# Running sums kept in PSUM between chunks by ScalarE copies, in place of VectorE adds in SBUF

## The chip, the cores and the metric

The kernel runs on one core of a Trainium2 chip, alone. The metric is device time in microseconds (us), the median of several executions; lower is better. The names of the engines in the profile are PE (TensorE, the matrix unit), DVE (VectorE), ACT (ScalarE), POOL (GpSimd) and SP (SyncE, which only issues transfers). A "q" behind a name (ACTq) is that engine's own instruction queue, which issues transfers and semaphore instructions.

## The reference

One layer of a network on x of 2048 rows and 576 columns. The rows are normalized, and two branches are added to x: a sliding, dilated attention and a two-layer MLP.

```python
xn = layernorm(x)
qkv = xn @ wqkv                      # 576 x 1728, 32 heads of 18
a = local_attention(qkv, window=8, dilation=2) @ wo
h = maximum(xn @ w1, 0)              # 576 x 4608
return x + a + h @ w2                # 4608 x 576
```

All of it is fp32. The kernel splits each operand into a high part and a rest (tiles hi and lo), both in a rounded fp32 form that the matrix unit takes at full rate, and multiplies three of the four pairs of parts.

## The kernel before, in words

The 2048 rows are taken in two phases of 1024. In a phase the rows lie in 8 tiles of 128 (index i), and two tiles make one of 4 row blocks (index tb). The 4608 hidden columns lie in 36 blocks of 128, and 3 blocks (index f) make one of 12 chunks (index c). A **slot** n is one (phase, c, tb, f), in this order from the outside in, so there are 288 slots, 144 in a phase, and f = n mod 3.

The tile X[phase, i] starts as x and collects every branch: it is the running sum, in SBUF. In slot n the main loop (lines 771 to 786) issues, in this order:

- run_splits(n): a part of a weight that has landed in SBUF is split by an ACT copy (hi) and a DVE subtraction (lo), lines 148 and 152;
- h_mm(n+2): the 14 matmuls of the first product two slots ahead, into a PSUM tile `ph`, and behind them h_out: an ACT relu into hhi (line 563) and a DVE operation that makes hlo (line 566);
- what the dictionary todo holds for slot n: tiles of the query, key and value product (qkv_tile), transposes of the next phase's x, the output projection of the attention (wo_b). The qkv_tile copies k, v and q out of PSUM on ACT (lines 397 to 399). The last of a unit's eight tiles also issues four transfers from ACT's queue (line 403), which copy the halo rows of k and v between partitions;
- o_mm(n): the 12 matmuls of the second product, 6 into PO[0] and then 6 into PO[1], one PSUM tile for each row tile of the block. Both tiles come from the pool ps_o, which has two buffers of two banks, so the next group's PO[0] lies where this group's lay;
- o_out(n), when f is 2: the three blocks of the chunk are summed in PO[0] and PO[1], and DVE adds each to its running sum (line 620);
- what todo_late holds, and run_bg: attention operations on DVE from a queue, as many as a count of planned DVE time (`t["dve"]`) against planned PE time (`t["pe"]`) admits. One of them is an exponential on ACT (line 444).

Each engine takes its instructions in the order in which the program issues them. Line 113 is the helper that issues every matmul, so the profile's rows of matmuls are told apart by their tiles: `ph` is the first product, `po` the second, `pm` the rest. A unit u of the attention has its eight qkv_tiles in slots 7+26u to 14+26u of each phase (u from 0 to 3). The attention's output projection lies in slots 127 to 137 of a phase; slots 139 to 143 of the first phase hold copies and subtractions (xt_s, lines 369 to 373) that split the next phase's x, which came back from memory transposed.

The last three slots write PO into other buffers and are finished in halves (lines 590 to 594 and 625 to 630).

Of the kernel before, what the change touches and what calls it, by code (L numbers as in the profile page):

```python
# [10 lines left out]
F32 = mybir.dt.float32  # L11
F32R = mybir.dt.float32r
AF = mybir.ActivationFunctionType
ALU = mybir.AluOpType
# [3 lines left out]
P = 128  # L18
# [7 lines left out]
C = 3  # L26
# [29 lines left out]
def tile_body(ctx: ExitStack, tc: tile.TileContext, x, wqkv, wo, w1, w2, out):  # L56
    nc = tc.nc
    S, D = x.shape
# [7 lines left out]
    D2 = D // 2  # L66
    CUT = (slice(0, 256), slice(256, D))
    scale = Dh ** -0.5
    SPC = NTB * C
# [20 lines left out]
    ps_o = pool("ps_o", 2, space=PSUM)  # L90
# [19 lines left out]
    t = {"pe": 0.0, "dve": 0.0}  # L110

    def mm(o, l, r, start, stop, n):
        nc.tensor.matmul(o, l, r, start=start, stop=stop)  # L113
        t["pe"] += n / 2400.0 + 0.002

    def dve(n):
        t["dve"] += (n + 130) / 960.0
# [119 lines left out]
    X, XT, XN, MR = {}, {}, {}, {}  # L237
# [144 lines left out]
    def qkv_tile(ph, u, i):  # L382
        if u == 0 and i == 0:
            QO[ph] = qop.tile([P, NI, D], F32, name="qo")
        if i == 0:
            assert len(bg) < 38, len(bg)
            KK[ph, u] = kp.tile([P, W - 1 + NI, UD], F32, name="k")
            VV[ph, u] = vp.tile([P, W - 1 + NI, UD], F32, name="v")
            nc.gpsimd.memset(KK[ph, u][0:1, 0 : W - 1, :], 0.0)
            nc.gpsimd.memset(VV[ph, u][0:1, 0 : W - 1, :], 0.0)  # L390
        k, v, wq = KK[ph, u], VV[ph, u], WQ[ph, u]
        tb, h = divmod(i, 2)
        xt = XT[ph, tb]
        pq = ps_m.tile([P, 3, UD], F32, name="pm")
        for j, (a, b) in enumerate(TERMS):
            mm(pq, xt[:, a, h * P : (h + 1) * P], wq[:, b, :], j == 0, j == len(TERMS) - 1, 3 * UD)
        nc.scalar.activation(k[:, W - 1 + i, :], pq[:, 1, :], AF.Copy)  # L397
        nc.scalar.activation(v[:, W - 1 + i, :], pq[:, 2, :], AF.Copy)
        nc.scalar.activation(QO[ph][:, i, u * UD : (u + 1) * UD], pq[:, 0, :], AF.Copy)
        if i == NI - 1:  # L400
            for z in (k, v):
                for a, b in HALO:
                    nc.scalar.dma_start(z[a + 1 : b + 1, 0 : W - 1, :], z[a:b, NI : NI + W - 1, :])
# [117 lines left out]
    def wo_b(ph, i):  # L521
        d, w = OT.pop((ph, i)), WO[ph]
        po = [ps_m.tile([P, c.stop - c.start], F32, name="pm") for c in CUT]
        for j, (a, b) in enumerate(TERMS):
            for h, c in enumerate(CUT):
                mm(po[h], d[a], w[b][:, c], j == 0, j == len(TERMS) - 1, D2)
        for h, c in enumerate(CUT):
            acc = X[ph, i][:, c]
            nc.vector.tensor_tensor(acc, po[h], acc, op=ALU.add)  # L529
            dve(D2)  # L530
# [3 lines left out]
    def done(ph, i):  # L534
        left[ph, i] -= 1
        if left[ph, i] == 0:
            nc.sync.dma_start(o_v[ph, i], X[ph, i])


    slots = [(ph, c, tb, f) for ph in range(NPH) for c in range(NCH) for tb in range(NTB) for f in range(C)]  # L540
    H, PO = {}, {}
# [3 lines left out]
    def h_terms(n, terms, other=False):  # L545
        ph, c, tb, f = slots[n]
        w, xt = W1[ph, c, f], XT[ph, tb]
        if n not in HP:
            HP[n] = ps_m.tile([P, TBN], F32, name="pm") if other else ps_h.tile([P, TBN], F32, name="ph")
            HN[n] = 0  # L550
        for a, b in terms:
            wb = w[:, b // 5, (b % 5) * P : (b % 5 + 1) * P]
            HN[n] += 1
            mm(HP[n], wb, xt[:, a, :], HN[n] == 1, HN[n] == len(TERMS), TBN)
# [24 lines left out]
    def half(po, h):  # L579
        if isinstance(po, list):  # L580
            return po[h]
        return po[:, 1, 0 : D - 256] if h else po[:, 0, 256:512]

    def o_mm(n, out=True, which=range(2)):
        ph, c, tb, f = slots[n]
        hi, lo = H[n]
        w = W2[ph, c, f]
        end = n == len(slots) - 1
        for k in which:
            if f == 0 and n == len(slots) - C:  # L590
                if k:
                    PO[k] = [ps_m.tile([P, c.stop - c.start], F32, name="pm") for c in CUT]
                else:
                    PO[k] = [ps_o.tile([P, 2, 512], F32, name="po")[:, 0, 0 : c.stop - c.start] for c in CUT]
            elif f == 0:
                PO[k] = ps_o.tile([P, 2, 512], F32, name="po")
            cs = slice(k * P, (k + 1) * P)
            terms = [(j, l, b, h) for j, (l, b) in enumerate(((hi, 0), (hi, 1), (lo, 0))) for h in range(2)]
            if end:
                terms.sort(key=lambda z: -z[3])  # L600
            for j, l, b, h in terms:
                mm(
                    half(PO[k], h), l[:, cs], w[:, b, CUT[h]],
                    f == 0 and j == 0, f == C - 1 and j == 2, D2,
                )
        if 1 in which:
            H.pop(n)
        if out:
            o_out(n, which)

    def o_out(n, which=range(2)):
        ph, c, tb, f = slots[n]
        if f < C - 1:
            return
        for k in which:
            i = 2 * tb + k
            acc = X[ph, i]
            if n < len(slots) - 1:
                whole = PO[k].rearrange("p b c -> p (b c)")[:, 256 : 256 + D]
                nc.vector.tensor_tensor(acc, whole, acc, op=ALU.add)  # L620
                dve(D)
                if c == NCH - 1:
                    done(ph, i)
                continue
            for h, c in reversed(list(enumerate(CUT))):
                nc.vector.tensor_tensor(acc[:, c], half(PO[k], h), acc[:, c], op=ALU.add)  # L626
                if k:
                    (nc.scalar if h else nc.sync).dma_start(o_v[ph, i][:, c], acc[:, c])
            if k == 0:
                done(ph, i)  # L630
# [13 lines left out]
    for ph in range(NPH):  # L644
        b = ph * SPP
# [93 lines left out]
    x2[1]()  # L739
    x2[3]()  # L740
    o_mm(0)
    o_mm(1)
    make_xt(0, 3, bank=ps_h)
    o_mm(2, out=False)
    stats(0, 4)
    s5 = stats(0, 5, parts=True)
# [6 lines left out]
    h4[0]()  # L753
    h4[1]()
    o_out(2, (0,))
    x4 = make_xt(0, 4, parts=True)
    for f in x4[:3]:
        f()
    norm(0, 5)
    o_out(2, (1,))  # L760
    x4[3]()
    h_terms(5, TERMS)
# [51 lines left out]
```

## Time and profile before

| | |
|---|---|
| time of the kernel, median of 3 runs (lowest, highest) | 1166.1 us (1165.38, 1167.42) |
| profiled execution, from its first to its last instruction | 1163.8 us |
| granted TensorE clock, mean | 0.999 |
| ACT copies and relus of 128x256 or more, from PSUM | 384 ns (256), 599 ns (512) |
| DVE add of a finished tile (line 620) | 190 of them, 757 ns each |

The profiled execution is one run with the hardware profiler on. Its page gives the span alone, 1163.8 us, so the median of the runs shown stands 2.3 us above it; what lies around the first and last instruction is in no row. A row of the timeline reads: start in us from the span's start, duration in us, engine, line, operation, written tile <- read tiles, shapes, count, and in brackets the idle time of the engine just before and what ended it. Where a row stands for several instructions, its duration runs from the first's start to the last's end. Matmuls overlap: the next starts before the last has ended, so the step from one group's start to the next is the time that counts. A row of a table of groups ends with: busy us, mean ns of one, idle us before them, and what ended that idle time.

### The profile page before, as it was taken

To read this page: it belongs to the slowest core of one execution; us is meant where nothing else is said; L and a number is where in the kernel's file an instruction comes from. 1 tells how busy PE (TensorE), PEld (TensorE's weight loads), DVE (VectorE), ACT (ScalarE), POOL (GpSimd) and SP (SyncE) were. 2 spreads that over 40 slices of the span, in tenths; PEclk is the share of its full clock that TensorE was granted. 3 is DMA by queue.
4 is the path that set the end of the run, shared out by engine and by line. 5 is a ranking of instruction groups with operands and counts; after the bars stand their busy time and mean duration, and the time that the engine had idled before them with its cause. 6 is when DMAs were issued, how large, how long until landed. Compare 5 with 4: busy or idle time off the path is not lost.

```text
span 1163.8 us, 21695 instructions
## 1 busy us (share of the span) xinstructions
PE 1155.9 (99%) x8916; PEld 1147.9 (99%) x8916; DVE 822.9 (71%) x1300; ACT 308.1 (26%) x747; POOL 44.9 (4%) x60
## 2 busy tenths in 40 slices
PE   8999999999999999999999999999999999999998
PEld 8999999999999999999999999999999999999998
DVE  7427885887687688876683288768858877887843
ACT  4422222131231212322433123222222312222210
POOL 2200100010000000000010001000100000000000
PEclk9999999999999999999999999999999999999999
DMA  6303221140321211365752113021312303113541
GB/s 184 98 23 85 65 55 53 40 112 1 94 76 34 82 32 52 96 151 116 175 170 66 46 53 94 22 77 36 92 34 62 110 1 101 44 32 97 123 100 63
DMA packets 149732, 88.66 MB, mean 76 GB/s; under 512 B 58512, under 2 KB 133264, under 8 KB 149632
## 3 DMA queue, kind: packets, MB, share of 16 engines
q1 hardware_dynamic: 146656, 78.54, 25.1%
q10 hardware_dynamic: 2976, 8.72, 2.6%
q8 instruction: 70, 1.15, 0.4%
q14 instruction: 30, 0.25, 0.1%
HBM read 67.90 MB, written 11.14 MB: 68 GB/s over the span
## 4 chain that ended last, share of the span: by engine, by line
PE 99%; issue 0%; DVE 0%; DMA 0%; POOL 0%; ACT 0%; SPq 0%; DVEq 0%; POOLq 0%
PE ph L113 39%; PE po L113 38%; PE pm L113 20%; PE pm L293 0%; DMA x<-in_x 0%; DVE x L626 0%; POOL rstd L264 0%; PE pm L294 0%; PE po L293 0%; ACT xT L298 0%; DVE xn L279 0%; DVE bst L257 0%; SPq L243 0%; DVEq L810 0%; PE ph L294 0%
## 5 line engine op out<-in xcount | busy, mean ns | idle before, releaser
L113 PE MATMUL ph<-xT,w1t 128*128 128x256 f32 x4018 | 505.0, 277 | 0.7 <-ACT xT L298 0.7
L113 PEld LDWEIGHTS ph<-xT,w1t 128*128 128x128 f32 x4018 | 486.8, 188 | 1.3 <-ACT xT L298 1.0
L113 PE MATMUL po<-w2t,hhi 128*128 128x256 f32 x2292 | 393.0, 293 | 0.0
L113 PEld LDWEIGHTS po<-w2t,hhi 128*128 128x128 f32 x2292 | 335.4, 188 | 1.1
L563 ACT ACTIVATE hhi<-ph 128x256 fp32r<-128x256 f32 x287 | 110.0, 384 | 582.2 <-PE ph L113 568.9
L113 PE MATMUL po<-w2t,hlo 128*128 128x256 f32 x1146 | 242.4, 292 | 0.0
L566 DVE SCALAR_TENSOR_TENSOR hlo<-ph,hhi 128x256 fp32r<-128x256 f32 x287 | 121.0, 422 | 164.5 <-ACT hhi L563 164.0
L113 PEld LDWEIGHTS po<-w2t,hlo 128*128 128x128 f32 x1146 | 188.9, 187 | 0.0
L620 DVE TENSOR_TENSOR x<-po,x 128x576 f32<-128x576 f32 x190 | 143.1, 757 | 60.1 <-PE po L113 57.2
L113 PE MATMUL pm<-wq,xT 128*128 128x432 f32 x896 | 185.5, 358 | 0.0
L113 PEld LDWEIGHTS pm<-wq,xT 128*128 128x128 f32 x896 | 163.8, 188 | 5.6
L428 DVE TENSOR_TENSOR pr<-qo,k 128x1152 f32<-128x1152 f32 x64 | 86.1, 1349 | 0.0
L431 DVE TENSOR_REDUCE lg<-pr 128x64 f32<-128x1152 f32 x64 | 85.1, 1343 | 0.0
L458 DVE TENSOR_TENSOR pr<-lg,v 128x1152 f32<-128x1152 f32 x64 | 84.7, 1350 | 0.0
L152 DVE TENSOR_TENSOR w2t<-st,w2t 128x576 fp32r<-128x576 f32 x72 | 55.8, 775 | 32.4 <-ACT w2t L148 32.3
L152 DVE TENSOR_TENSOR w1t<-st,w1t 128x640 fp32r<-128x640 f32 x70 | 58.9, 841 | 20.6 <-ACT w1t L148 20.5
L465 DVE TENSOR_TENSOR pr<-pr 128x288 f32<-128x288 f32 (+1 forms) x128 | 70.6, 601 | 0.0
L148 ACT ACTIVATE w2t<-st 128x576 fp32r<-128x576 f32 x72 | 49.3, 684 | 44.9 <-PE po L113 32.5
L397 ACT ACTIVATE k<-pm 128x144 f32<-128x144 f32 x64 | 18.7, 292 | 146.3 <-PE pm L113 146.3
L148 ACT ACTIVATE w1t<-st 128x640 fp32r<-128x640 f32 x71 | 52.1, 734 | 11.7 <-DMA k<-k 6.0
L434 POOL TENSOR_SCALAR_AFFINE_SELECT lg<-lg 1x512 f32<-1x512 f32 x8 | 9.9, 1234 | 809.6 <-DVE lg L431 809.6
L529 DVE TENSOR_TENSOR x<-pm,x 128x256 f32<-128x256 f32 (+1 forms) x32 | 13.1, 453 | 30.2 <-PE pm L113 30.2
(85 smaller groups left out, 470.0 us busy)
## 6 DMA issues: line engine op xcount, KB each, us to landing
st<-in_w SPq DMA_DIRECT2D x72, 288.0 KB, 3.1
st<-in_w SPq DMA_DIRECT2D x72, 256.0 KB, 3.2
st<-in_wqkv SPq DMA_DIRECT2D x32, 216.0 KB, 3.0
turned<-tr SPq DMA_DIRECT2D x64, 80.0 KB, 3.0
xn<-turned SPq DMA_DIRECT2D x16, 320.0 KB, 3.2
st<-in_w SPq DMA_DIRECT2D x142, 32.0 KB, 2.9
out<-x SPq DMA_DIRECT2D x15, 288.0 KB, 2.1
x<-in_x SPq DMA_DIRECT2D x14, 288.0 KB, 4.3
```

What stands on the lines that cost most here:

```text
L113: nc.tensor.matmul(o, l, r, start=start, stop=stop)
L148: nc.scalar.activation(hi, src, AF.Copy)
L152: nc.vector.tensor_tensor(lo, src, f32(hi), op=ALU.subtract)
L397: nc.scalar.activation(k[:, W - 1 + i, :], pq[:, 1, :], AF.Copy)
L428: nc.vector.tensor_tensor(pr[i], q, window(k, i), op=ALU.mult)
L431: nc.vector.tensor_reduce(lg[:, i], pr.pop(i).rearrange(heads, d=Dh), axis=AX.X, op=ALU.add)
L458: nc.vector.tensor_tensor(pr[i].rearrange(heads, d=Dh), e, window(v, i).rearrange(heads, d=Dh), op=ALU.mult)
L465: nc.vector.tensor_tensor(o, z[:, 0:n], z[:, n : 2 * n], op=ALU.add)
L529: nc.vector.tensor_tensor(acc, po[h], acc, op=ALU.add)
L563: nc.scalar.activation(hi, pt, AF.Relu)
L566: nc.vector.scalar_tensor_tensor(lo, pt, 0.0, f32(hi), op0=ALU.max, op1=ALU.subtract)
L620: nc.vector.tensor_tensor(acc, whole, acc, op=ALU.add)
```

## The change

Three things change. In the groups of slots from 12 to 284 the first matmul into PO no longer starts a new accumulation. The PSUM tile is written ahead by ACT: as soon as a group is finished, o_out takes the next group's PO[k] and copies the running sum of that group's row tile into it (the seed). And when a group is finished, ACT copies PO[k] back to the running sum (the copy back), where DVE added before. The order on ACT at a group's end is: copy back of k = 0, seed of k = 0, copy back of k = 1, seed of k = 1. The first chunk of the first phase and the last group keep their DVE adds: 182 of the 190 adds of line 620 go, and 182 copies back and 182 seeds come, at 91 ends of groups (slots 14 to 284 for the copies, 11 to 281 for the seeds). The planned DVE time of these adds leaves the count that run_bg uses.

```diff
-        nc.tensor.matmul(o, l, r, start=start, stop=stop)
+        nc.tensor.matmul(o, l, r, start=start, stop=stop, skip_group_check=True)
...
+    def seeded(n):
+        return SPC <= n < len(slots) - C
+
...
-            elif f == 0:
+            elif f == 0 and not seeded(n):
                 PO[k] = ps_o.tile([P, 2, 512], F32, name="po")
...
-                    f == 0 and j == 0, f == C - 1 and j == 2, D2,
+                    f == 0 and j == 0 and not seeded(n), f == C - 1 and j == 2, D2,
...
                 whole = PO[k].rearrange("p b c -> p (b c)")[:, 256 : 256 + D]
-                nc.vector.tensor_tensor(acc, whole, acc, op=ALU.add)
-                dve(D)
+                if seeded(n):
+                    nc.scalar.activation(acc, whole, AF.Copy)
+                else:
+                    nc.vector.tensor_tensor(acc, whole, acc, op=ALU.add)
+                    dve(D)
+                if seeded(n + 1):
+                    after = slots[n + 1]
+                    PO[k] = ps_o.tile([P, 2, 512], F32, name="po")
+                    whole = PO[k].rearrange("p b c -> p (b c)")[:, 256 : 256 + D]
+                    nc.scalar.activation(whole, X[after[0], 2 * after[2] + k], AF.Copy)
                 if c == NCH - 1:
                     done(ph, i)
```

## The prediction

> **What bounds the kernel now.** I read the first page first (busy shares and the chain that ended last), then the groups by shape, then the timeline around the ends of groups.
>
> ```profile
> span 1163.8 us, 21695 instructions
> PE 1155.9 (99%) x8916; PEld 1147.9 (99%) x8916; DVE 822.9 (71%) x1300; ACT 308.1 (26%) x747; POOL 44.9 (4%) x60
> ...
> PE 99%; issue 0%; DVE 0%; DMA 0%; POOL 0%; ACT 0%; SPq 0%; DVEq 0%; POOLq 0%
> ```
>
> PE is busy for 99% of the span, and the chain that ended last lies on PE for 99%. So PE is the bound, and nothing waits on DVE that PE then waits on. A busy PE could still be slowed by DVE's traffic; two stretches of one slot each test that (columns: length; busy time and count of PE, PEld, DVE, ACT, POOL; granted clock; DMA share and GB/s):
>
> ```profile
> 85.54:88.71 3.17, 3.17 (x28) 3.17 (x26) 1.52 (x2) 0.66 (x3) 0.00 (x0) 1.00 0.45 117
> ...
> 98.17:101.32 3.15, 3.15 (x29) 3.15 (x27) 3.15 (x4) 1.01 (x2) 0.00 (x0) 1.00 0.00 0
> ```
>
> A slot takes 3.17 us with DVE busy for 1.52 and 3.15 us with DVE busy throughout. PE doesn't notice DVE. Taking work off DVE can therefore win nothing that these rows show. What remains is the question whether ACT can do the new work in time.
>
> **The change part by part.** First the prices:
>
> ```profile
> L563 ACT ACTIVATE hhi<-ph 128x256 fp32r<-128x256 f32 x287 | 110.0, 384 | 582.2 <-PE ph L113 568.9 <-DMA k<-k 12.3 <-DVE w2t L152 0.8
> ...
> L620 DVE TENSOR_TENSOR x<-po,x 128x576 f32<-128x576 f32 x190 | 143.1, 757 | 60.1 <-PE po L113 57.2
> ...
> L148 ACT ACTIVATE w2t<-st 128x576 fp32r<-128x576 f32 x72 | 49.3, 684 | 44.9 <-PE po L113 32.5 <-DMA st<-in_w 6.2 <-DMA k<-k 5.9
> ...
> L298 ACT ACTIVATE xT<-pm 128x512 fp32r<-128x512 f32 x11 | 6.6, 599 | 5.0 <-PE pm L293 4.7
> ...
> L344 ACT ACTIVATE pr<-pr,rstd 128x576 f32<-128x576 f32 x4 | 3.1, 778 | 0.4
> ```
>
> *Removed:* 182 DVE adds of 757 ns, 138 us of DVE; worth nothing on the path. DVE falls to about 685 us. The attention operations that run_bg then issues earlier fill DVE's free time, which PE doesn't notice either.
>
> *Copy back,* PSUM to SBUF, 576 columns: from 384 ns at 256 columns and 599 ns at 512 the step is 0.84 ns a column, so 599 + 64 x 0.84 = 653 ns.
>
> *Seed,* SBUF to PSUM, 576 columns: no row shows ACT writing PSUM. The nearest is the same size from SBUF to SBUF, 684 ns, and I take it. Upper bound: 778 ns, the dearest row of 576 columns, which has a scale read per row. Lower bound: 600 ns, about what 512 columns from PSUM take (599). A pair is 0.653 + 0.684 = 1.337 us; 182 pairs are 243 us, and ACT goes to about 551 us, 47%. As a share that is no bound. What counts is where the pairs fall.
>
> *The added wait.* PE now can't start the next group's k = 0 until the first seed is written, nor its k = 1 until the second is. Before, it waited for the two adds. All of PE's later work is queued behind these matmuls, so each us of wait is a us of the result. On ACT the pairs stand behind the relu and all else that slot issued, and ahead of the next splits and relu. A plain end of a group (PE rows, then ACT):
>
> ```profile
> 104.47 0.68 PE L113 MATMUL po<-w2t,hhi 128*128 128x256 f32 x4
> 104.99 0.42 PE L113 MATMUL po<-w2t,hlo 128*128 128x256 f32 x2
> ...
> 106.03 1.76 PE L113 MATMUL ph<-xT,w1t 128*128 128x256 f32 x14
> 107.63 0.68 PE L113 MATMUL po<-w2t,hhi 128*128 128x256 f32 x4
> ...
> 108.41 0.68 PE L113 MATMUL po<-w2t,hhi 128*128 128x256 f32 x4
> ```
> ```profile
> 104.67 0.38 ACT L563 ACTIVATE hhi<-ph 128x256 fp32r<-128x256 f32 x1 [2.14 <-PE ph L113]
> 104.95 0.68 ACT L148 ACTIVATE w2t<-st 128x576 fp32r<-128x576 f32 x1
> ```
>
> The k = 0 sum is finished at 104.99 + 0.42 = 105.41. The relu ends at 105.05, so ACT is free; the w2t split behind it belongs to the next slot and would now follow the pairs. With 0.04 us from release to start (at slot 14, below, the sum is finished at 86.07 + 0.42 = 86.49 and the waiting add starts at 86.53), the chain is: copy back 105.45, seed 106.10 to 106.79, copy back to 107.44 (k = 1 is long finished), seed to 108.12; with 0.04, PE may go on with k = 0 at 106.83 and with k = 1 at 108.16. It wants them at 107.63 and 108.41. Both are hidden beside h_mm and the k = 0 matmuls, **by 0.80 and only 0.25 us.** The displaced splits and relu come up to 2.7 us later, but feed matmuls two slots on, and a slot is 3.15 us: nothing.
>
> That order costs in two kinds of place. **First, the halo transfers.** They are issued by ACT just ahead of o_out where slot 14+26u has f = 2: u = 0 and u = 3, in both phases, four times.
>
> ```profile
> 86.06 0.61 ACTq L403 DMA_DIRECT2D k<-k  x1
> ...
> 86.71 1.39 ACTq L403 DMA_DIRECT2D k<-k  x1
> 88.19 1.43 ACTq L403 DMA_DIRECT2D v<-v  x2
> 89.72 0.39 ACT L563 ACTIVATE hhi<-ph 128x256 fp32r<-128x256 f32 x1 [3.33 <-DMA k<-k]
> ```
> ```profile
> 86.53 1.54 DVE L620 TENSOR_TENSOR x<-po,x 128x576 f32<-128x576 f32 x2 [2.69 <-PE po L113]
> ```
> ```profile
> 86.07 0.42 PE L113 MATMUL po<-w2t,hlo 128*128 128x256 f32 x2
> ...
> 87.11 1.76 PE L113 MATMUL ph<-xT,w1t 128*128 128x256 f32 x14
> 88.71 0.68 PE L113 MATMUL po<-w2t,hhi 128*128 128x256 f32 x4
> ...
> 89.48 0.68 PE L113 MATMUL po<-w2t,hhi 128*128 128x256 f32 x4
> ```
>
> ACT issues until 89.62 and starts its next work at 89.72. DVE had finished the adds at 88.07. In the new kernel the pairs take the relu's place: 89.72 + 1.337 + 0.04 = 91.10 for k = 0, wanted at 88.71, a stall of 2.39 us; 89.72 + 2.674 + 0.04 = 92.43 for k = 1, wanted at 89.48: late by **2.95 us** in all. The other three, with ACT's first work after the issue and PE's k = 1:
>
> ```profile
> 401.39 0.68 ACT L148 ACTIVATE w2t<-st 128x576 fp32r<-128x576 f32 x1 [2.96 <-DMA k<-k]
> ...
> 663.25 0.39 ACT L563 ACTIVATE hhi<-ph 128x256 fp32r<-128x256 f32 x1 [2.99 <-DMA k<-k]
> ...
> 975.19 0.69 ACT L148 ACTIVATE w2t<-st 128x576 fp32r<-128x576 f32 x1 [2.90 <-DMA k<-k]
> ```
> ```profile
> 401.52 0.68 PE L113 MATMUL po<-w2t,hhi 128*128 128x256 f32 x4
> ...
> 663.35 0.68 PE L113 MATMUL po<-w2t,hhi 128*128 128x256 f32 x4
> ...
> 975.39 0.68 PE L113 MATMUL po<-w2t,hhi 128*128 128x256 f32 x4
> ```
>
> By the same sum they are late by 2.58, 2.61 and 2.51 us. **The four make 10.65 us.**
>
> **Second,** slots 140 and 143 have three xt_s copies on ACT ahead of o_out; the last of them, and PE's k = 1 of the next group:
>
> ```profile
> 579.73 0.31 ACT L373 ACTIVATE xT<-xT 64x128 fp32r<-64x128 f32 x1
> ...
> 589.57 0.31 ACT L373 ACTIVATE xT<-xT 64x128 fp32r<-64x128 f32 x1
> ```
> ```profile
> 582.23 0.69 PE L113 MATMUL po<-w2t,hhi 128*128 128x256 f32 x4
> ...
> 592.37 0.68 PE L113 MATMUL po<-w2t,hhi 128*128 128x256 f32 x4
> ```
>
> 580.04 + 2.71 = 582.75 against 582.23, and 589.88 + 2.71 = 592.59 against 592.37: 0.52 + 0.22 = 0.74 us.
>
> Where the next slot holds a qkv_tile (19 of the 91 ends), its 14 long matmuls come ahead of o_mm and hide more. This holds at slot 11 too, where the seeds wait for DVE adds. The attention's exponential also holds ACT until DVE gets to its input:
>
> ```profile
> ACT lg L444 <- DVE lg L443: 17.2, 4, 5.3
> ```
>
> That is 4 waits in 1164 us. run_bg admits attention work behind an f = 1 slot only up to 1.5 us past PE's planned time (M, line 769), so that ACT should be through before the chain of the f = 2 slot starts. I cost it at nothing; a wait that hits a chain in full would cost about what a halo end costs, and the upper end of the range has room for two or three.
>
> *What is moved:* the output transfer and SP's queue now wait for the copy back instead of the add, some tenths of a us apart; they are off the path. The skipped start of an accumulation is a flag, at no cost.
>
> Sum: 10.65 + 0.74 = 11.4 us. The span becomes 1163.8 + 11.4 = 1175.2, and with the 2.3 us of the median above the span **1177.5 us**, 1.0% slower.
>
> On back-to-back work, the relu above runs to 105.05 and the split starts at 104.95, an overlap of 0.10 us. The Trainium skill, ScalarE: Activation LUTs, "What ACT_TABLE_LOAD costs", says that such ACTIVATEs overlap by about 93 ns; the trace agrees for two that are independent. By it each chain of four would be 0.28 us shorter, and the sum would be 11.4 - 6 x 0.28 = 9.7 us, an estimate. I leave the overlap out, because a seed overwrites what the copy back ahead of it reads; the next rows show a dependent pair, with a gap of 0.10 us instead:
>
> ```profile
> 546.13 0.76 ACT L343 ACTIVATE pr<-x,nm 128x576 f32<-128x576 f32 x1
> 546.99 0.78 ACT L344 ACTIVATE pr<-pr,rstd 128x576 f32<-128x576 f32 x1
> ```
>
> So a chain is between 0.30 shorter (three overlaps) and 0.20 longer (two gaps). With overlaps and seeds of 600 ns it is 0.30 + 2 x 0.084 = 0.47 shorter: four halo ends of 8.8 us and the two others at nearly nothing, 1175 us.
>
> **The rivals.**
>
> *Plain ends stall too.* With seeds at 778 ns and two gaps of 0.10 us a chain is 0.19 + 0.20 = 0.39 longer, and the slack of 0.25 turns into a wait of 0.14 at each plain end. Of the 91 ends, 19 have a qkv_tile behind them, 3 transposes, 4 the halo issue, 1 the copies of slot 140; 64 are left: 9.0 us. The six places above grow by 6 x 0.39 = 2.3 us. Together 11.4 + 11.3 = 22.7, or 1188.8 us. For it speaks the thin slack; against it, that it takes nearly both upper bounds at once.
>
> *Not slower: the halo issue doesn't hold the pairs.* If ACT ran the pairs beside the issue, the 10.65 us would vanish and 0.74 be left: 1166.8 us, no change that can be told. It decides at an issue that blocks ACT for less than about 0.25 us beyond the finished k = 0 sum. Against it: the relu at 89.72 needed nothing of k, its matmuls (the 87.11 row) had ended at 88.87, and it started only when the issue was over; the other three rows name the same releaser.
>
> *PE's clock drops after the stalls.* If the granted clock were halved for one slot of 3.15 us after each of the four stalls, that would add 12.6: 1190 us. Against it:
>
> ```profile
> 6.00:12.00 6.00, 3.23 (x22) 2.51 (x23) 4.42 (x12) 3.08 (x7) 3.16 (x3) 1.00 0.93 279
> ```
>
> In the head PE is idle for 2.8 of 6 us and the granted clock stays at 1.00. The Trainium skill, TensorE: Matmul & The Clock Gate, "Part 1: The HAM clock gate", gives the half clock after an idle window of about 3.4 us; stalls of about 2.4 us would stay below it. The trace agrees, for gaps that short.
>
> **How the numbers follow.** My forecast (halo ends and xt_s alone, 1175 to 1180) has 0.62; plain ends stalling too, wholly or in part, 0.20; the clock 0.04; an issue that doesn't hold the pairs 0.08; a gain that no row of before shows 0.06. The forecast and the two dearer rivals are slower by over 0.2%, which is about what a measurement of this kernel tells from no change; 0.08 is the same; 0.06 faster. Slower holds 0.86. The range goes from 1172 (below the cheapest chain, since the lengths of the issue vary between the four rows) to 1191 (plain ends at their bound, or the clock).
>
> **What would show it.** DVE busy near 685 us and ACT near 551; seeds as a group of 182 on ACT writing `po`, of 600 to 778 ns. PE's waits: `po` released by ACT, about 11 us in six places, four of them with a longest gap of 2.0 to 2.4 us at slots 15, 93, 159 and 237, and none at plain ends. It is wrong if PE shows no wait behind the halo issue, or if waits of tenths of a us repeat every 9.5 us through the whole span; seeds over about 0.8 us would do the latter.

## The result and the profile after

The changed kernel takes 1186.5 us (median of 4 runs, 1183.31 to 1188.73) against 1165.74 us before (4 runs, 1165.06 to 1167.42): a ratio of 1.0172, 95% interval 1.015 to 1.0194. That is 20.8 us, where 11.4 were forecast. The profiled execution spans 1183.4 us, 19.6 more than before; its own time was 1185.2 us, 1.8 above its span.

The page of the changed kernel, busy times:

```profile
span 1183.4 us, 21959 instructions
PE 1165.0 (98%) x8916; PEld 1153.0 (97%) x8916; DVE 690.2 (58%) x1118; ACT 525.4 (44%) x1111; POOL 43.6 (4%) x60
```

Its groups, for the matmuls and the two new lines (the last figures of a row are the idle time ahead of the group, and what ended it):

```profile
L113 PE MATMUL ph<-xT,w1t 128*128 128x256 f32 x4018 | 507.4, 277 | 3.4 <-DVE hlo L566 2.4
...
L113 PE MATMUL po<-w2t,hhi 128*128 128x256 f32 x2292 | 395.8, 294 | 9.0 <-ACT po L632 9.0
...
L624 ACT ACTIVATE x<-po 128x576 f32<-128x576 f32 x182 | 117.1, 644 | 67.3 <-PE po L113 52.7
L632 ACT ACTIVATE po<-x 128x576 f32<-128x576 f32 x182 | 119.4, 656 | 6.8 <-DVE x L626 0.9
```

The work went where it should: DVE is at 690 us (685 forecast), ACT at 525 (551). The copy back takes 644 ns (653), the seed 656 (684). What is new is the idle time on PE. Its waits (us in total, times, longest):

```profile
ACT lg L444 <- DVE lg L443: 27.7, 8, 4.9
...
PEld po L113 <- ACT po L632: 11.7, 12, 2.4
...
PE po L113 <- ACT po L632: 9.0, 11, 2.2
...
PEld ph L113 <- DVE hlo L566: 4.1, 6, 1.2
...
PE ph L113 <- DVE hlo L566: 2.4, 4, 1.0
```

Two kinds. PE waits for seeds, as forecast, and it waits for `hlo`, the DVE half of the first product's output, which nobody forecast. The first row belongs to the second kind: all eight exponentials of the attention now hold ACT, four did before.

**A plain end,** in the timeline of the changed kernel, ACT and then PE:

```profile
109.12 0.65 ACT L624 ACTIVATE x<-po 128x576 f32<-128x576 f32 x1 [0.40 <-PE po L113]
109.80 0.66 ACT L632 ACTIVATE po<-x 128x576 f32<-128x576 f32 x1
110.39 0.64 ACT L624 ACTIVATE x<-po 128x576 f32<-128x576 f32 x1
111.06 0.66 ACT L632 ACTIVATE po<-x 128x576 f32<-128x576 f32 x1
```
```profile
111.29 0.68 PE L113 MATMUL po<-w2t,hhi 128*128 128x256 f32 x4
...
112.07 0.68 PE L113 MATMUL po<-w2t,hhi 128*128 128x256 f32 x4
```

The chain runs from 109.12 to 111.72, PE wants its end at 112.07, and the slack is 0.31 us (0.04 for the release). The seed starts 0.03 us after the copy back that it depends on, and the next copy back, which depends on nothing, overlaps the seed by 0.07.

**A halo end,** slots 14 and 15:

```profile
85.87 1.39 ACTq L403 DMA_DIRECT2D k<-k  x1
87.36 1.43 ACTq L403 DMA_DIRECT2D v<-v  x2
88.83 0.65 ACT L624 ACTIVATE x<-po 128x576 f32<-128x576 f32 x1 [3.28 <-DMA k<-k]
89.52 0.65 ACT L632 ACTIVATE po<-x 128x576 f32<-128x576 f32 x1
...
90.77 0.66 ACT L632 ACTIVATE po<-x 128x576 f32<-128x576 f32 x1
```
```profile
86.28 1.76 PE L113 MATMUL ph<-xT,w1t 128*128 128x256 f32 x14
90.22 0.79 PE L113 MATMUL po<-w2t,hhi 128*128 128x256 f32 x4 [2.19 <-ACT po L632]
...
91.48 1.33 PE L113 MATMUL po<-w2t,hhi 128*128 128x256 f32 x4 [0.20 <-ACT po L632]
...
93.09 2.60 PE L113 MATMUL ph<-xT,w1t 128*128 128x256 f32 x14
95.53 0.68 PE L113 MATMUL po<-w2t,hhi 128*128 128x256 f32 x4
```

Undisturbed, 14 matmuls into ph step on by 1.60 us and 6 into po by 0.78. So k = 0 was due at 87.88 and came 2.34 later, and k = 1 was due 0.78 behind it and came another 0.48 later: 2.82 us, forecast 2.95. But the next two steps are too long as well, by 0.83 and 0.84 us, though PE waits for nothing there: the 14 matmuls take 2.60 us instead of 1.76. Windows around this place, around the second halo end and over the wait of the third (length; busy time and count of PE, PEld, DVE, ACT, POOL; granted clock; DMA share and GB/s):

```profile
88.02:91.43 3.41, 1.07 (x7) 0.82 (x6) 0.00 (x0) 2.53 (x5) 0.00 (x0) 1.00 0.57 176
91.43:94.84 3.41, 3.36 (x15) 3.36 (x16) 0.42 (x1) 0.30 (x1) 0.00 (x0) 0.50 0.00 0
...
405.46:408.87 3.41, 1.60 (x14) 1.40 (x13) 0.00 (x0) 2.01 (x4) 0.00 (x0) 1.00 0.78 235
408.87:412.28 3.41, 3.41 (x15) 3.08 (x14) 2.10 (x4) 2.70 (x5) 0.00 (x0) 0.50 0.08 22
...
671.70:675.11 3.41, 2.68 (x23) 2.48 (x21) 0.00 (x0) 0.53 (x3) 0.00 (x0) 1.00 0.64 183
675.11:678.52 3.41, 2.14 (x14) 1.91 (x15) 0.42 (x1) 2.50 (x5) 0.00 (x0) 1.00 0.38 117
```

The granted clock was halved for 3.41 us behind the first halo end; it was so behind the second too, and not behind the third and fourth. The two dips start 317.44 us apart, which is 93 times 3.41, and in every profiled execution here the changes of the clock lie whole steps of 3.41 us apart. On these steps the four places differ, though PE's waits hardly do (2.19, 1.81, 1.79 and 1.80 us): PE was idle for 2.34 and 1.81 us of the step ahead of the two dips. The third wait lies across two steps, 0.73 and 1.27 us of each idle, and the fourth has 1.60 us in one.

**An exponential,** in the timeline of the changed kernel around slot 106 (DVE, ACT, PE):

```profile
448.73 1.16 DVE L440 TENSOR_REDUCE m<-lg 128x64 f32<-128x512 f32 x1 [1.61 <-POOL lg L434]
449.92 0.69 DVE L443 TENSOR_TENSOR lg<-lg,m 128x512 f32<-128x512 f32 x1
...
453.35 0.42 DVE L566 SCALAR_TENSOR_TENSOR hlo<-ph,hhi 128x256 fp32r<-128x256 f32 x1
```
```profile
450.70 0.63 ACT L444 ACTIVATE lg<-lg 128x512 f32<-128x512 f32 x1 [2.30 <-DVE lg L443]
...
452.45 0.36 ACT L563 ACTIVATE hhi<-ph 128x256 fp32r<-128x256 f32 x1
```
```profile
453.83 1.87 PE L113 MATMUL ph<-xT,w1t 128*128 128x256 f32 x14 [0.97 <-DVE hlo L566]
```

ACT stands at the exponential until DVE has done the maximum and the subtraction; DVE waited 1.61 us for POOL before them. Behind the exponential come two weight splits, then the relu, then DVE's hlo, and PE can't reuse the `ph` buffer before.

To account for the span, the starts of PE's groups were set against those of before, slot by slot. What is added, in us:

| place | waits for | added |
|---|---|---|
| slots 15, 93, 159, 237 | the seed behind the halo issue | 2.82 + 2.46 + 2.43 + 2.44 = 10.15 |
| right behind these four | lowered clock at two of them; slow first matmuls behind a wait at all four | 1.67 + 1.44 + 0.13 + 0.12 = 3.36 |
| slots 57, 107, 201, 251 | hlo, behind an exponential | 0.71 + 1.25 + 0.68 + 0.87 = 3.51 |
| slots 81, 225 | the seed, ACT late behind an exponential | 0.96 + 0.96 = 1.92 |
| slot 120 | the seed, ACT late behind two splits that waited for weights | 0.50 |
| slot 141 | the seed behind the xt_s copies | 0.46 |
| slots 30, 151, 174 | | 0.35 |

Together 20.25; the head of this execution was 0.77 us quicker, and 19.5 of the 19.6 us are told. Plain ends cost nothing.

### The profile page after: what moved, and what is told of

Its sections match the earlier page's. It is cut to its first block, busy times and chain, and to the rows that moved or that the text cites. A ratio compares the mean times of both kernels' runs of the same rounds, so it can differ in the third digit from the quotient of the medians.

```text
span 1183.4 us, 21959 instructions
## 1 busy us (share of the span) xinstructions
PE 1165.0 (98%) x8916; PEld 1153.0 (97%) x8916; DVE 690.2 (58%) x1118; ACT 525.4 (44%) x1111; POOL 43.6 (4%) x60
## 3 DMA queue, kind: packets, MB, share of 16 engines
q8 instruction: 70, 1.15, 0.4%
## 5 line engine op out<-in xcount | busy, mean ns | idle before, releaser
L624 ACT ACTIVATE x<-po 128x576 f32<-128x576 f32 x182 | 117.1, 644 | 67.3 <-PE po L113 52.7
L632 ACT ACTIVATE po<-x 128x576 f32<-128x576 f32 x182 | 119.4, 656 | 6.8 <-DVE x L626 0.9
```

The costliest lines, as they stand in the source:

```text
L624: nc.scalar.activation(acc, whole, AF.Copy)
L632: nc.scalar.activation(whole, X[after[0], 2 * after[2] + k], AF.Copy)
```

## The experiments

The theory after this reading has three parts: the halo issue ahead of the pairs on ACT's queue (10.2 us), a lowered clock behind such waits (about 3 us), and run_bg's count, which lost the 182 adds and therefore issues the attention earlier, where its exponentials meet the rest badly (5.4 us). The rival to the third part is that ACT is simply fuller, whatever the count. Each experiment has its own runs of the kernel before on the same chip; the medians of these were 1166.96 (e1 to e4), 1167.58 (e5, e6) and 1167.28 us (e7, e8).

**e1_plan**

```diff
                 if seeded(n):
                     nc.scalar.activation(acc, whole, AF.Copy)
+                    dve(D)
```

> The changed kernel, with the planned DVE time of the 182 removed adds left in the count that run_bg uses, so that the attention operations stand where they stood before. Theory (the plan's shift moved the eight exponentials, ACT and DVE wait for each other around them, and PE waited 5.4 us in slots 57, 81, 107, 201, 225 and 251): those waits go, the halo waits stay, 1178 to 1182 us. Rival (ACT's fuller queue alone makes these waits, the plan has no part in it): waits of the same kind and size stay, 1185 to 1188 us.

1181.87 us (4 runs, 1176.77 to 1183.34), ratio 1.0125 (1.0101 to 1.015). The exponentials stand where they stood before the change, only two of them still hold ACT, and PE's waits for hlo are gone from the list:

```profile
ACT lg L444 <- DVE lg L443: 10.2, 2, 5.3
PEld po L113 <- ACT po L633: 10.2, 8, 2.4
...
PE po L113 <- ACT po L633: 8.5, 8, 2.2
```

In the starts of PE's groups, slots 57, 81, 107, 201, 225 and 251 add nothing. The four halo ends come 2.4 to 3.1 us late, as in the changed kernel. The rival falls. ACT's wait alone isn't the price either: at 464.07 us of this execution an exponential still holds ACT for 5.28 us, but two relus follow it at once, no splits, and PE doesn't wait. The profiled execution also shows where much of the spread of the runs comes from: the first three halo ends are each followed by a dip of the clock, the fourth is not, and a fourth dip lies in the head. The windows of the second, the third and the fourth halo end are means, with 3.41 us at 0.50 in each of the first two:

```profile
410.00:415.00 5.00, 5.00 (x30) 5.00 (x30) 3.10 (x6) 2.13 (x5) 0.00 (x0) 0.66 0.40 106
675.00:680.00 5.00, 4.46 (x21) 4.23 (x22) 0.42 (x1) 1.82 (x4) 0.00 (x0) 0.66 0.13 44
...
995.00:1000.00 5.00, 5.00 (x43) 5.00 (x43) 4.26 (x7) 1.95 (x4) 0.00 (x0) 1.00 0.75 202
```

Of the four runs, the one with a mean granted clock of 1.000 took 1176.77 us, those at 0.994 to 0.996 took 1181.35 to 1183.34. In the changed kernel it was 1183.31 at 1.000 and 1187.8 and 1188.73 at 0.994.

**e2_halo_sp**

```diff
-                    nc.scalar.dma_start(z[a + 1 : b + 1, 0 : W - 1, :], z[a:b, NI : NI + W - 1, :])
+                    nc.sync.dma_start(z[a + 1 : b + 1, 0 : W - 1, :], z[a:b, NI : NI + W - 1, :])
```

> The changed kernel, with the four halo transfers of each unit issued from SP's queue instead of ACT's. Theory (four waits of 2.4 to 2.8 us behind the issue, 10.2 us, 0.12 us of refilling behind each, and about 1.4 us of lowered clock behind a wait where it occurs): 1171 to 1174 us, granted clock 0.999 or more in every run, runs within 0.3% of each other. Rival on the clock (it dips by itself, not because PE stood idle): the waits go, but clocks of 0.994 to 0.997 stay in some runs and 1172 to 1178 us. Rival on the queue (the issue doesn't hold the pairs): no change, 1186 us.

1172.75 us (1171.57 to 1173.55), ratio 1.0053 (1.0036 to 1.007); clocks 0.999 to 1.000 in all four runs, which lie within 0.2% of each other. Slots 15, 93, 159 and 237 add nothing; the places of the exponentials add what they added in the changed kernel. Both rivals fall: the issue did hold the pairs, and the clock did dip because PE stood idle there.

**e3_plan_halo_sp** has both edits.

> Both edits: the old plan count and the halo transfers from SP. Theory: what is left is 0.5 us at slot 141 and some tenths, 1166 to 1168 us, within 0.2% of the kernel before. Rival (ACT's fuller queue makes the other waits): 1171 to 1174 us.

1168.62 us (10 runs, 1166.11 to 1169.79), ratio 1.0014 (1.0005 to 1.0023). That is 0.6 above the expected 1168. The two edits together take the ratio from 1.0172 to 1.0014, and the lowered clocks behind the halo ends are gone. In its profiled execution slot 120 adds 0.48, slot 141 0.46 and slot 151 0.13 us. The rest of the distance lies in the head, ahead of any pair, where this execution ran 2.7 us behind the one of before: PE waited 2.16 us there for the first normalized rows, and the granted clock was 0.50 from 8.77 to 15.60. Means over two windows there:

```profile
5.00:10.00 5.00, 2.68 (x18) 2.17 (x17) 2.61 (x7) 1.74 (x3) 1.07 (x3) 0.88 0.83 237
10.00:15.00 5.00, 4.32 (x20) 3.86 (x19) 3.73 (x10) 2.25 (x5) 3.24 (x3) 0.50 0.97 323
```

The kernel before has such runs as well: at a mean clock of 0.997 it took 1167.82 and 1168.03 us, at 1.000 from 1164.88 to 1165.92. The three runs of e3 at 1.000 took 1166.11 to 1166.69.

**e4_seed_twice**

```diff
                     nc.scalar.activation(whole, X[after[0], 2 * after[2] + k], AF.Copy)
+                    if k == 0:
+                        nc.scalar.activation(whole, X[after[0], 2 * after[2] + k], AF.Copy)
```

> The changed kernel, with the seed of k = 0 written twice, one more ACT copy of 656 ns in each of the 91 chains. Theory (plain ends have 0.31 us of slack by the rows of the changed kernel, then each further us is a us of PE): 64 plain ends wait 0.29 to 0.35 us and refill for 0.12, 26 to 30 us, and some ten places that wait already grow by 0.65: 1216 to 1224 us. Rival (the chains have ample cover): only the places that wait already grow, 1191 to 1194 us.

1232.98 us (1230.79 to 1236.27), ratio 1.0574 (1.0554 to 1.0593), dearer than either expected. The slack is as thin as read: PE now waits for the seed 69 times instead of a dozen, and k = 1 of a plain end comes 0.36 to 0.38 us late. What was sized too low is the time behind a wait. PE in slots 42 and 43:

```profile
206.35 0.81 PE L113 MATMUL po<-w2t,hhi 128*128 128x256 f32 x4 [0.19 <-ACT po L632]
...
207.27 1.82 PE L113 MATMUL ph<-xT,w1t 128*128 128x256 f32 x14
208.93 0.70 PE L113 MATMUL po<-w2t,hhi 128*128 128x256 f32 x4
```

From 206.35 to the next group it takes 0.92 instead of 0.78, and the 14 matmuls step on by 1.66 instead of 1.60. The slow steps go on for two slots, until 213.78, at a granted clock of 1.00:

```profile
207.00:210.00 3.00, 3.00 (x27) 3.00 (x26) 3.00 (x4) 1.10 (x3) 0.00 (x0) 1.00 0.00 0
```

So this end cost 0.38 + 0.13 + 0.2, about 0.7 us for a wait of 0.38. The one at slot 24 cost 0.38 + 0.10 and nothing more. Why some are followed by slow steps and others not wasn't settled.

**e5_plan_halo_late** takes e1 and issues the transfers from ACT behind the pairs of the same slot:

```diff
+            late(s + NI - 1, halo, ph, u)
             late(s + NI + 1, attention, ph, u)
```

> The changed kernel with the old plan count, and the four halo transfers issued by ACT as before, but behind the pairs of the same slot instead of ahead of them. Theory (the order on ACT's queue makes the halo waits, not the issue itself): the four waits behind the issue go, and what ACT does late behind it (relu, splits) has two slots of cover: 1167 to 1171 us. Rival (the issue time of 3.1 to 3.5 us comes back as late relus and PE waits for ph): waits of PE on hlo at slots 16 to 18 and 94 to 96, 1173 to 1180 us.

1170.56 us (10 runs, 1168.14 to 1172.33), ratio 1.0028 (1.0016 to 1.004). Same queue, same issue, other order: the waits for seeds at the four halo ends are gone. The rival has a part all the same: at slots 95 and 239, where weight splits stand between the issue and the relu, PE comes 1.11 and 1.75 us late for hlo. The first:

```profile
407.56 1.92 PE L113 MATMUL ph<-xT,w1t 128*128 128x256 f32 x14 [0.78 <-DVE hlo L567]
```

**e6_plan_halo_half** takes e1 and leaves the transfers of k on ACT, those of v on SP:

```diff
-                    nc.scalar.dma_start(z[a + 1 : b + 1, 0 : W - 1, :], z[a:b, NI : NI + W - 1, :])
+                    (nc.scalar if z is k else nc.sync).dma_start(z[a + 1 : b + 1, 0 : W - 1, :], z[a:b, NI : NI + W - 1, :])
```

> The changed kernel with the old plan count, and of the four halo transfers the two of k issued by ACT, the two of v by SP. ACT is then held until about 2.0 us past the first matmul of the slot's second product instead of 3.7 to 4.1, so that the chain ends about 0.7 us late in place of 2.4 to 2.8. Theory (the wait is the issue time beyond the cover, and the clock dips only behind waits of about 2 us): four waits of 0.5 to 0.9 us, clock at 1.00 behind them, 1169 to 1173 us. Rival (any wait of PE lowers the clock): clock of 0.65 to 0.9 in some of the windows behind the four, 1173 to 1178 us.

1171.46 us (6 runs, 1170.1 to 1172.79), ratio 1.0036 (1.0025 to 1.0048). The wait scales with the issue: 1.29, 0.73, 0.74 and 0.73 us late. The first, on PE, and the window over it:

```profile
89.63 0.80 PE L113 MATMUL po<-w2t,hhi 128*128 128x256 f32 x4 [0.65 <-ACT po L633]
...
90.89 0.80 PE L113 MATMUL po<-w2t,hhi 128*128 128x256 f32 x4 [0.19 <-ACT po L633]
```
```profile
90.00:95.00 5.00, 4.81 (x39) 4.57 (x38) 1.42 (x3) 1.49 (x4) 0.00 (x0) 1.00 0.73 185
```

The clock stays at 1.00 behind all four; the longest of these waits is 0.65 us.

**e7_before_plan** is the kernel before, with its DVE adds, and the count of the changed kernel:

```diff
                 nc.vector.tensor_tensor(acc, whole, acc, op=ALU.add)
-                dve(D)
+                if not SPC <= n < len(slots) - C:
+                    dve(D)
```

> The kernel before, with its DVE adds, but with the planned DVE time of the 182 adds left out of the count that run_bg uses, so that the attention operations stand where the changed kernel has them. Theory (the plan's shift alone puts the exponentials where ACT and DVE hold each other, and here DVE has the adds to do besides): waits of PE for hlo at the same slots as in the changed kernel, or larger, and some for the adds, 1170 to 1185 us. Rival (the shift hurts only together with the pairs on ACT): 1165 to 1168 us.

1191.4 us (1190.58 to 1192.74), ratio 1.0204 (1.0187 to 1.0221): more than the whole change cost, without a single pair on ACT. PE comes late above all at slots 30, 56, 57, 81, 107, 174, 200, 201, 225 and 251, by 1.3 to 3.9 us each:

```profile
ACT lg L444 <- DVE lg L443: 50.3, 8, 6.8
PEld ph L113 <- DVE hlo L566: 13.8, 10, 2.7
PE ph L113 <- DVE hlo L566: 11.5, 10, 2.4
PE po L113 <- DVE x L620: 6.1, 8, 1.5
```

The places of the changed kernel are among them. The clock was halved for 3.41 us behind two of these waits too (2.42 us, at slot 107, and 2.07, at 251), and stayed at 1.00 behind the others, the longest of them 1.54 us. Here DVE has the uncounted adds to do besides, so the size doesn't carry over; that the count alone places the exponentials badly does.

**e8_before_halo_sp** is the kernel before, with the edit of e2.

> The kernel before, with the four halo transfers of each unit issued from SP's queue. Theory (the issue time on ACT is covered where DVE does the adds, so moving it wins nothing, and what moving it won in the changed kernel is the wait of the pairs alone): 1165 to 1168 us. Rival (SP's queue is a better place in any case): 1161 to 1164 us.

1167.88 us (10 runs, 1165.51 to 1168.52), ratio 1.0002 (0.9993 to 1.0012). Nothing: where DVE does the adds, the issue on ACT is covered, and what e2 won was the wait of the pairs.

No version beat the kernel before. That follows from the first page: with PE busy for 99% of the span, a freed DVE has nothing to give.

## Why the prediction was right, and where its sum was too small

The 1186.5 us lies inside the range of 1172 to 1191, but above the 1175 to 1180 on which most of the chance lay. The range reached so far up for plain ends that stall and for a clock halved behind all four halo ends; the first didn't happen, the second happened at half of the places and at half the price. It also had room for two or three exponentials that hit a chain in full; there were six smaller hits. That these costs together still lie inside the range is luck in part.

- **PE is the bound and DVE's relief wins nothing.** Right. With both costs taken away (e3) the changed kernel comes to 1.0014 of before, not below it.
- **The pairs fit at plain ends, by 0.25 us.** Right: 0.31 us, and no plain end waits. The prices were 653 and 684 ns for 644 and 656. The rival that plain ends stall didn't happen, and e4 shows that 0.66 us more on the chain would have made it happen.
- **The halo transfers hold the pairs: 10.65 us.** Right in mechanism, places and size: 10.15 us, moved away by e2 and, with the issue on the same queue, by e5. The rival that the issue doesn't hold them fell.
- **The xt_s copies: 0.52 + 0.22 us.** 0.46 at slot 141 and nothing at slot 144.
- **The attention's new places: "I cost it at nothing".** This is the step that failed. The argument was that behind an f = 1 slot run_bg admits work only up to 1.5 us past PE's planned time. The count holds neither DVE's waits for POOL (10.3 us in 8 waits in the changed kernel) nor ACT's wait for DVE, and the changed kernel issues its exponentials behind slots 27, 53, 78, 104 and the same of the second phase, all with f = 0 or 2, where M admits 3.0 us. Even in the kernel before the four exponentials that held ACT were issued behind slots 59, 108, 203 and 252, none with f = 1, so the limit did not guard them there. The new places cost 5.4 us at six places; e1 takes them away, e7 makes them without the pairs.
- **The clock, at a chance of 0.04.** It happened, at a smaller price than the rival's: 1.3 to 1.6 us behind a halo wait, at two of four in the profiled execution. A halved clock for 3.41 us of time costs at most half of that, 1.7 us; the rival had counted 3.15. The row that spoke against it, a head with 2.8 idle us of 6 at a clock of 1.00, was one execution; in the one of e3 the clock fell to 0.50 in the same head. PE was idle for 1.68 and 1.15 us of two steps of 3.41 us in the first, without a dip, and for 1.88 us of the step ahead of the dip in the second. The Trainium skill, TensorE: Matmul & The Clock Gate, "Part 1: The HAM clock gate", puts the half clock behind an idle window of about 3.4 us. The runs agree with the half clock and show dips of 3.41 us, but they disagree on the idle time: 1.81 and 2.34 us of a step were enough behind the two halo waits.

The sum had 11.4 us. At a mean clock of 1.000 the run of e1, which has the old count, stands 11 to 12 us above the runs of before at that clock (1176.77 against 1164.88 to 1165.92). The count's 5.4 us and about 3 us of lowered clock make most of the rest.

## What to carry to other kernels

When work is moved between engines, look at what the receiving engine's queue holds just ahead of it: the halo transfers' issue at four places, harmless for as long as nothing urgent stood behind it, cost more than the 364 new copies. A hand-kept count of an engine's time is part of the schedule; taking an operation out of it moves everything that the count admits, and that has to be priced or held fixed. And when the bound is an engine that is busy for 99%, price a relief of another engine at zero first, and then look for what the move can break.

## What the runs showed of the hardware

- Where ACT's queue issued four transfers it was held for 3.2 to 3.6 us (eight places in each of before and after), and no activation behind them started meanwhile.
- The granted clock fell to 0.50 for 3.41 us behind nine of the 14 PE waits of 1.78 to 2.88 us that the profiled executions of the changed kernel, e1, e4 and e7 show past the head, and behind none of up to 1.54 us. What tells the nine apart is mostly how a wait lies on the steps of 3.41 us on which the clock changes: PE was idle for 1.76 to 2.75 us of the step ahead of a dip, and for at most 1.60 us of one with no dip behind it, except for one of 1.91 us in e4. In the heads the border is less clear (1.55 us with a dip in e4, 1.73 without in e6). Why is not shown.
- These dips are much of the spread of the runs: in those of before beside e1 to e4, 1164.88 to 1165.92 us at a mean clock of 1.000, 1167.82 and 1168.03 at 0.997.
- Behind a short wait PE was slow to resume: 0.14 us over the next six matmuls in slot 42 of e4, at a granted clock of 1.00, and in some places about 3% over the next two slots (1.66 us instead of 1.60 for 14 matmuls).
- ACT from SBUF to PSUM took 656 ns for 576 columns, 28 ns less than the 684 of a split's copy from SBUF to SBUF in the kernel before, which also rounds its output.
